# A new order of 1190 planned steps, other engines for 47 evacuations, and a new table of array parts

## The chip, the cores and the metric

The kernel runs on one core of one Trainium2 chip. Five engines work side by side on it: TensorE (PE; matmuls and transposes, with weight loads on PEld beside them), VectorE (DVE), ScalarE (ACT), GpSimd (POOL) and SyncE (SP), which here issues most of the DMAs. The metric is device microseconds of one execution; lower is better. Each engine takes its own instructions strictly in the order in which the program gives them and waits on semaphores for what it needs from the others.

## The reference

One input `x` of 2048 rows by 640 channels is normalised over its channels. The normalised rows go two ways: through a gated long convolution (A) and through a feed-forward net (B). The product of the two, through a SiLU, is added to `x`.

```python
def _A_ref(q, k, v, shift_k, ssm_k, ssm_D):
    ...
    for t in range(ks):                       # ks = 4
        k_shift = k_shift + k_pad[:, t:t + S, :] * shift_k[:, ks - 1 - t][None, None, :]
    kv = k_shift * v
    ...
    kv_f = rfft(kv, padded to 2 S)            # S = 2048
    kf_f = rfft(ssm_k, padded to 2 S)
    y = irfft(kv_f * kf_f)[:S] + kv * ssm_D
    return q * y

def _B_ref(x, w1, b1, w2, b2):                # 640 -> 1728 -> 640
    return einsum(gelu(einsum(x, w1) + b1), w2) + b2

xn = layernorm(x)
return x + _A_ref(xn, k, v, ...) * silu(_B_ref(xn, ...))
```

(The two transforms are shortened to words here.) B_x is not used.

## The kernel before

The long convolution is done by a transform of length 4096 split into two stages. The first stage multiplies 128 x 128 matrices of cosines and sines (`WA`, `WB`) onto the rows; the second multiplies 32 x 32 matrices (`mats`) onto blocks of 32 rows; between the two stages the data change places through DRAM. So there are three trips through DRAM: `scrK` (the filter's spectrum), `scrU` (the signal's) and `scrC` (the product on its way back). On each trip all 16 stores have to land before any of the 16 loads can run, because each load reads a stripe of every store.

The feed-forward net runs over four chunks of 512 rows. Chunk 0 is taken up by a fixed opening (`prologue`), which also does the first six hidden blocks of that chunk. Everything after it is a list of 1190 names, `PLAN`, that is read from left to right; each name calls one small function and issues its instructions. The order of the list is thus the order on every engine's queue and on SP's and GpSimd's DMA queues. Nothing else orders the work: an engine that reaches an instruction too early waits there, and everything behind it on that engine waits too.

The names that matter here (a number is the piece, `.a` or `.d` says ScalarE or VectorE):

- `h`, `he`: one hidden block of 128 features of the feed-forward net, five matmuls of 512 columns (L463; every 14th, `h13 h27 h41 h55`, is a narrow one, L459), and its gelu on ScalarE (L475, L472). Numbers 0 to 13 are chunk 0, 14 to 27 chunk 1, and so on.
- `g`, `ge`, `gm`: one output half-block, 14 matmuls of 320 columns (L496), its SiLU on ScalarE (L504), the product on VectorE (L511). A `g` needs all 14 `he` of its chunk and all of `w2_sb`.
- `ls lv lr lb ln`: layernorm (statistics L417, L418 on VectorE; the root on GpSimd L426; the normalisation on ScalarE L438 or VectorE L440). `tt`, `te`: four transposes of normalised rows (L447), evacuation.
- `em`, `ee`: matmuls that spread the four taps over the partitions (L641), evacuation into `w_exp`. `cv`: one multiplication, addition or product with `v` of the short convolution, on VectorE (L590, L586, L579), eight to each of eight pieces.
- `w`, `ws`: phases and sines that fill `WA` and `WB`; `s ss sm` the same for `mats`; `d` adds `ssm_D` into the filter (L638).
- `kt`, `kc`: five transposes of one sixteenth of the filter, one from each of its five loads (L535), evacuation. `kf`, `ke`, `ks`: first stage of the filter (L546), evacuation, store to `scrK` on GpSimd's queue (L561). `uf`, `ue`, `us`: the same for the signal (L546, L572).
- `fl`: load of a `scrK` pair on SP (L595). `ff`, `fe`: 32-row unit of the filter's second stage, evacuation. `ml`: load of a `scrU` pair (L652). `mk`: two loads that swap even and odd partitions of the filter's spectrum (L658). `mu`: 32-row unit of the signal. `mp`, `mq`: two products of spectra on VectorE, straight from PSUM (L670). `ma`, `mb`: the two 32-row units of the inverse, into one bank. `me`: evacuation. `ms`: store to `scrC` (L700).
- `ip ia is ib ic`: `WA` and `WB` are filled anew for the way back. `yl`: load of `scrC` (L707). `y`, `yt`: last stage (L715, L716) and product with the normalised rows (L724). `yo`, `ys`: addition of `x` and store for the first three chunks; `ga`, `gs` for the last.
- `X B C K V q`: loads of `x`, `w2`, the filter, `k`, `v`, and `x` again (L238, L272 to L275, L268, L243 to L245, L248, L704), all on SP. `B2` is three small loads, `C` five of 512 KB.

Two kinds of storage are handed out while the list is read: eight PSUM banks (`ones`) and 48 row-pair slots of one large SBUF tile (`slots`). Both are first-in-first-out: a step that opens a new piece takes the one that has been free for longest, and the step that uses a piece for the last time gives its place back. So a new order also changes which bank and which slot each piece gets, and on whose last use it waits. In the opening the six blocks of the prologue hold banks 0 to 5, and 6 and 7 are free.

The second-stage units (`ff mu ma mb`, 192 in all) use a 32 x 32 corner of the array for each block of rows, four matmuls a unit. The digit of `TURNS` for the unit's number (0 to 47) says which column block is paired with which row block (L408 to L410): digit t pairs block i with i+t. Forward units (`ff`, `mu`) and inverse ones (`ma`, `mb`) swap the roles of the two, so units whose pairings differ can run in the array at the same time.

All evacuations go through one helper (`evac`), L146 where ScalarE does it and L147 where VectorE does it. ScalarE keeps one table of functions loaded: gelu, or SiLU, which serves the sines too; `use_table` issues a change where the list demands one.

Of the kernel before, what the change touches and what calls it, by code (L numbers as in the profile page):

```python
# [39 lines left out]
kt4 kt3 kt13 kf25 kt9 kf34 kt2 V6 kc14.a kc3.a kc13.d kc4.d ke34.a kc2.d kt12 kf0 kc9.d kc12.d ke25.a kf33 ke0.a  # L40
ke33.a kt10 kf6 kt7 V4 X2 V0 X3 kf2 kt6 kf7 kf17 kc7.a kc10.d ke6.d kf28 ke2.a kc6.a kf27 kt15 kf29 kt1 ke7.d kf12
ke17.d ke28.a ke29.a kf30 kc15.d kc1.d ke12.d ke27.a kf45 kf35 ke35.a kf15 kf39 kf31 kf20 ke39.a ke15.a kf8 ke30.a
ke45.a ke20.a ke8.a g3 cv33 ks11 ks9 kf13 cv13 cv40 cv23 ke31.d kf26 kf38 ge3 ke13.a ke38.a kf32 ke32.a ke26.a kf41
ke41.a kf47 kf37 gm3.d kf36 ke47.a ke36.a kf3 g4 gm2.d ke3.a ke37.a ge4 kf10 kf40 kf14 kf18 kf16 ke10.a kf19 ke40.a
ke16.a ke14.a ke19.a g5 kf44 kf5 kf46 kf23 kf24 cv14 cv56 cv5 cv34 cv35 cv48 cv24 cv41 cv15 kf1 ks10 ks12 ks2 ks5 ks13
cv42 cv43 gm4.d cv6 cv36 cv7 cv44 ke18.a ge5 ke46.a ke44.a g6 kf21 ks4 ks6 cv37 cv25 cv45 cv38 ke23.a ke24.a ke5.a
ke1.a ke21.a ks8 kf9 ke9.a kf4 kf11 kf22 ke22.a ge6 kf42 ke42.a ke11.a ke4.a g7 kf43 ge7 ke43.a uf4 uf14 ks15 uf3 uf13
ue3.a ue4.a uf12 uf16 uf5 ue14.a ue16.d cv39 ks7 ks0 ks1 ks3 cv46 cv26 cv57 cv49 cv27 ue12.a ue5.a h23 h18 h24 uf2
cv50 cv51 cv47 cv52 cv28 ue13.a he24 he18 uf29 uf9 ue29.a uf8 uf10 ue10.a ue9.a ue8.a h21 uf24 uf6 h16 uf26 ue2.a he23
he21 ue24.a he16 h14 uf1 uf7 ue7.a h26 he14 he26 ue26.a ue6.a uf34 h17 ue34.a uf33 h22 he17 ue1.a cv53 gm6.d cv54 cv58  # L50
cv29 uf28 uf17 h27 uf11 ue28.a he27 he22 h25 ue33.d ks14 fl6 fl4 fl2 fl10 fl12 fl8 fl1 fl5 fl9 cv55 cv59 ue11.a ue17.a
uf0 uf30 ue30.a ue0.d cv30 cv60 h20 he20 uf27 uf41 ue27.a uf35 uf36 h19 uf25 fl3 fl14 ue35.a he25 ue41.a uf38 uf37
fl11 fl0 us1 us4 us11 us2 h15 fl15 ue36.d he19 gm5.d cv31 fl7 ue38.d uf20 uf18 ue25.a uf31 uf23 uf19 he15 ls10 ls9
# [5 lines left out]
lb2 g11 ml4 ml3 ls14 fe34.a ln8.d ln10.d ln9.d ls15 ff25 ff11 ff10 ff5 ff38 ff16 g12 ge11 fe5.a fe10.a fe11.a fe25.a  # L59
fe16.a ge12 ln11.d fe38.d ff43 ff33 ff19 ff20 tt14 tt12 ff12 ff47 fe33.d fe19.a fe43.a mk3 ml1 fe20.d te14.d te12.d  # L60
tt13 fe12.a fe47.a ff4 fe4.a tt11 ff15 ff3 mu8 gm10.d lv3 mu7 ff26 g14 gm11.d gm12.d te11.a fe3.a fe15.a fe26.a te13.a
mk4 ml8 mk1 mu6 mp7 mp8 mq8 mq7 ma7 ma8 ff32 lr3 mb8 mu11 mu9 mb7 fe32.a lb3 tt10 g13 mk8 me8.a te10.a ln13.a me7.a
mp6 mp9 mq9 mp11 mq11 ml0 fl13 mu12 mq6 mk0 ml6 ff45 ff21 mu3 mu5 ge13 fe45.a ln15.a ge14 mp12 fe21.a mq12 mp5 g15 mq5
ge15 ma12 ff18 ma11 mb12 ma5 mp3 mq3 ml7 mb11 mu4 mu25 mb5 fe18.a me11.a me12.a me5.a h29 mu14 mp4 mu13 mu10 h32 he29
he32 mp25 mq25 mp10 h30 he30 mq10 mq4 mp13 mp14 mq14 mq13 h39 ln12.a mu1 ml5 ff30 ma9 mu26 mb9 ma4 h40 mp1 he39 mq1
fe30.a me9.a he40 mu2 mb4 mu18 ma6 ff39 h28 ml10 mk6 mk5 ml12 ml9 ml13 mk7 me4.a fe39.a mb6 ff36 mu24 mu19 ln14.a mp26
mk9 mq26 mp2 mp18 mq2 h34 h31 mp19 mp24 mq24 me6.a fe36.a he28 mk12 he34 mu15 mu17 mq19 ml14 mq18 he31 ff41 ma10 ma2
ff40 mb2 mb10 mu23 mp17 mq17 fe40.a me10.a me2.a fe41.a h35 h41 he35 mp15 mq15 he41 mp23 mq23 ma13 mu28 ma18 mb18 mu22
mb13 me13.a me18.a mp22 mq22 mp28 h36 he36 ma15 ma1 mb1 mb15 mu16 ma24 mb24 me15.a me1.a me24.a ml11 q6 h37 mp16 mq16
mu21 ma14 ma26 mq28 mb26 mk13 ma16 mb16 mb14 mu0 he37 q1 mu38 h38 me14.a me16.a me26.a he38 mp21 mq21 mp38 mp0 mq0 h33  # L70
mq38 ma19 ma0 q3 mk11 mk14 q7 ma3 mu27 mk10 gm14.d mu37 mu40 mb3 mb19 he33 mb0 tt18 te18.a me3.a me19.a me0.a g17 mp40
mp27 mq40 mq27 tt15 tt19 mp37 gm13.d mu20 mu34 mu41 mq37 g16 te15.a te19.a mp20 mp41 mq20 mq41 ma28 ma38 ma40 mu43
mb28 mb38 mb40 tt17 mk15 mp34 ml15 ge16 ge17 te17.a gm16.d mp43 gm17.d gm15.d g18 mu29 me38.a me40.a me28.a mq34 ma25
mu35 ma34 ma27 mb34 mu31 mb25 ge18 ms0 ms4 ms1 ms2 mb27 mq43 tt16 me34.a me27.a me25.a te16.a mp29 mp31 mp35 mq29 mq31
g19 ir mu39 ma29 mu36 ma17 ma31 ge19 mu32 mb29 mb17 mb31 mq35 me17.a me31.a me29.a ms5 g20 mp36 mq36 mp39 mq39 ma23
mu45 ma36 ma37 mb23 ma21 mb37 mb36 ge20 mu30 mb21 mp32 mq32 g21 ma20 mp30 me37.a me36.a me21.a me23.a mu47 ma39 ms3
ma41 mp45 mq30 mu33 ma30 mq45 gm19.d mb41 mb39 mb20 mb30 me39.a gm18.d me20.a g22 me41.a q0 ma43 mp33 mp47 q2 mq33
me30.a ge21 mq47 ma22 ma33 mu44 mu46 ma47 mb33 mb22 ge22 mb43 h53 me43.a me22.a ms9 mp44 me33.d mp46 mq44 ma32 ma35
# [828 lines left out]
```

## Time and profile before

| quantity | value |
|---|---|
| time, median of 3 runs | 196.9 us (196.85 to 197.02) |
| span of the profiled execution | 195.1 us |
| TensorE busy | 186.0 us, 95% of the span |
| VectorE busy | 174.9 us, 90% |
| ScalarE busy | 161.8 us, 83% |
| GpSimd busy | 49.3 us, 25% |
| moved by DMA | 57.69 MB, mean 296 GB/s |
| changes of ScalarE's table behind the opening | 7 |

The profiled execution is one run of the same program with the hardware profiler on; its span goes from the first instruction to the last. Start times in the rows are counted from the span's start. In rows that group instructions, "x14" is the number of instructions, and the name behind "<-" in brackets is what the engine last waited for. A TensorE row's length contains the time in which a matmul is still on its way through the array, so rows overlap; in the chain of work that ended last the overlaps are taken out. The granted clock is TensorE's, 1.00 for full speed.

### The profile page before, as it was taken

To read this page: it belongs to the slowest core of one execution; us is meant where nothing else is said; L and a number is where in the kernel's file an instruction comes from. 1 tells how busy PE (TensorE), PEld (TensorE's weight loads), DVE (VectorE), ACT (ScalarE), POOL (GpSimd) and SP (SyncE) were. 2 spreads that over 40 slices of the span, in tenths; PEclk is the share of its full clock that TensorE was granted. 3 is DMA by queue.
4 is the path that set the end of the run, shared out by engine and by line. 5 is a ranking of instruction groups with operands and counts; after the bars stand their busy time and mean duration, and the time that the engine had idled before them with its cause. 6 is when DMAs were issued, how large, how long until landed. Compare 5 with 4: busy or idle time off the path is not lost.

```text
span 195.1 us, 5140 instructions
## 1 busy us (share of the span) xinstructions
PE 186.0 (95%) x1927; PEld 110.8 (57%) x1939; DVE 174.9 (90%) x374; ACT 161.8 (83%) x320; POOL 49.3 (25%) x85
## 2 busy tenths in 40 slices
PE   7899979899999999999999999999999999999992
PEld 2486447776775555563556433356665454676771
DVE  6969999999999999999999999999999910479994
ACT  3467999989999999999998999989867699993031
POOL 8545300003555000635020000008073610002130
PEclk9999999999999999999999999999999999999999
DMA  6999999983599899987699998599897659994064
GB/s 199 386 363 312 348 392 404 401 349 154 202 368 364 292 337 364 397 328 288 235 300 307 312 363 295 174 281 352 254 304 304 238 190 315 369 392 186 5 234 171
DMA packets 26401, 57.69 MB, mean 296 GB/s; under 512 B 3016, under 2 KB 14857, under 8 KB 26376
## 3 DMA queue, kind: packets, MB, share of 16 engines
q1 hardware_dynamic: 21872, 39.65, 59.4%
q0 software_dynamic: 4320, 17.70, 24.1%
q8 instruction: 15, 0.25, 0.5%
q14 instruction: 10, 0.08, 0.1%
q10 hardware_dynamic: 184, 0.01, 0.1%
HBM read 33.76 MB, written 18.35 MB: 267 GB/s over the span
## 4 chain that ended last, share of the span: by engine, by line
PE 78%; DVE 16%; issue 2%; POOL 1%; ACT 1%; POOLq 0%; DVEq 0%; ACTq 0%
PE banks L496 28%; PE banks L463 22%; PE banks L546 9%; PE banks L410 9%; DVE area L590 3%; PE banks L535 2%; PE banks L715 2%; PE banks L716 2%; DVE area L586 2%; DVE st L417 2%; PE banks L447 2%; DVE stats L744 1%; DVE area L303 1%; DVE area L147 1%; DVE xnT L147 1%
## 5 line engine op out<-in xcount | busy, mean ns | idle before, releaser
L146 ACT CAST area<-banks 128x426 bf16<-128x426 f32 (+2 forms) x169 | 76.7, 570 | 5.4 <-PE banks L410 4.3
L496 PE MATMUL banks<-w_sb,hT 128*128 128x320 bf16 (+1 forms) x462 | 65.5, 295 | 0.0
L463 PE MATMUL banks<-xnT,w_sb 128*128 128x512 bf16 x218 | 53.2, 380 | 0.7 <-issue 0.2
L496 PEld LDWEIGHTS <-hT 128*128 128x128 bf16 x462 | 43.5, 98 | 18.2 <-issue 2.2
L670 DVE TENSOR_TENSOR area<-banks,area 128x426 bf16<-128x426 f32 (+1 forms) x96 | 49.9, 591 | 0.4 <-PE banks L410 0.4
L475 ACT ACTIVATE hT<-banks,b_f 128x512 bf16<-128x512 f32 x52 | 34.2, 708 | 2.5 <-PE banks L782 1.4
L463 PEld LDWEIGHTS <-w_sb 128*128 128x128 bf16 x230 | 21.3, 98 | 25.6 <-issue 3.6
L504 ACT ACTIVATE sl<-banks 128x320 bf16<-128x320 f32 (+1 forms) x33 | 14.7, 456 | 13.7 <-PE banks L496 11.2
L590 DVE TENSOR_TENSOR area<-area 128x1280 bf16<-128x1280 bf16 x32 | 24.8, 813 | 0.2
L700 POOL DMA_DIRECT2D scrC<-area x16 | 11.7, 733 | 41.6 <-ACT area L146 41.4
L410 PE MATMUL banks<-area,mats 32*32 32x426 bf16 (+1 forms) x768 | 20.9, 345 | 0.5
L724 DVE TENSOR_TENSOR area<-banks,xn 128x426 bf16<-128x426 f32 (+1 forms) x18 | 10.2, 592 | 12.3 <-ACT hT L475 11.3
L586 DVE TENSOR_TENSOR area<-area 128x1280 bf16<-128x1280 bf16 x24 | 18.9, 812 | 0.0
L561 POOL DMA_DIRECT2D scrK<-area x16 | 8.8, 555 | 29.7 <-ACT area L146 29.7
L546 PE MATMUL banks<-area,WA 128*128 128x428 bf16 (+1 forms) x64 | 16.1, 298 | 0.2
L410 PEld LDWEIGHTS <-mats 32*32 32x32 bf16 x768 | 8.1, 88 | 12.7 <-issue 9.6
L546 PE MATMUL banks<-area,WB 128*128 128x214 bf16 (+1 forms) x64 | 15.1, 299 | 0.0
L147 DVE CAST area<-banks 128x426 bf16<-128x426 f32 (+2 forms) x27 | 14.9, 583 | 0.0
L572 POOL DMA_DIRECT2D scrU<-area x16 | 8.6, 539 | 22.6 <-ACT area L146 20.7
L733 POOL DMA_DIRECT2D out_dram<-area x6 | 3.3, 547 | 28.6 <-DMA area<-in_A_q_dram 19.3
L417 DVE BATCH_NORM_STATS2 st<-xn 128x6 f32<-128x320 bf16 x24 | 10.3, 470 | 0.0
L511 DVE TENSOR_TENSOR xn<-xn,sl 128x320 bf16<-128x320 bf16 (+1 forms) x33 | 9.7, 308 | 0.4 <-ACT sl L504 0.4
(107 smaller groups left out, 202.3 us busy)
## 6 DMA issues: line engine op xcount, KB each, us to landing
scrK<-area POOLq DMA_DIRECT2D x16, 320.0 KB, 3.5
scrU<-area POOLq DMA_DIRECT2D x16, 320.0 KB, 4.0
area<-scrK SPq DMA_DIRECT2D x16, 320.0 KB, 6.0
area<-area SPq DMA_DIRECT2D x32, 160.0 KB, 4.1
area<-scrU SPq DMA_DIRECT2D x16, 320.0 KB, 5.9
scrC<-area POOLq DMA_DIRECT2D x16, 320.0 KB, 4.2
area<-scrC SPq DMA_DIRECT2D x16, 320.0 KB, 7.4
area<-in_A_k_dram SPq DMA_DIRECT2D x4, 640.0 KB, 8.2
```

Source lines behind the costliest of these rows:

```text
L146: return nc.scalar.copy(out=out_ap, in_=in_ap)
L147: return nc.vector.tensor_copy(out=out_ap, in_=in_ap)
L410: nc.tensor.matmul(out=out[b, :], lhsT=mats[a, m, a], rhs=rhs[a, :], start=start, stop=stop)
L417: nc.vector.bn_stats(out=st[:, j, h, :], in_=xn_tiles[c][:, j, h * HALF:(h + 1) * HALF])
L463: nc.tensor.matmul(out=ps, lhsT=w1_sb[:, t, ft * P:(ft + 1) * P], rhs=xnT[:, t, :], start=(t == 0), stop=(t == DT - 1))
L475: nc.scalar.activation(out=hT[:, ft, :], in_=one(("h", i)), func=ACT.Gelu_apprx_tanh, bias=b1_f[:, ft:ft + 1], scale=1.0)
L496: nc.tensor.matmul(out=ps[:, 0:ws.stop - ws.start], lhsT=hT[0:M, ft, q * P:(q + 1) * P], rhs=w2_sb[0:M, ft, hs.start + ws.start:hs.start + ...
L504: nc.scalar.activation(out=sl[:, ws], in_=one(key)[:, 0:ws.stop - ws.start], func=ACT.Silu)
L546: nc.tensor.matmul(out=ps[:, dst], lhsT=(WA, WB)[r][:, n2, :], rhs=rows[:, n2 % 2, src], start=True, stop=True)
L586: nc.vector.tensor_tensor(out=uc, in0=uc, in1=tmp, op=ALU.add)
L590: nc.vector.tensor_tensor(out=tmp if s else uc, in0=kh[:, r0:r0 + KC, :], in1=w_exp[:, j:j + 1, :].to_broadcast([P, KC, D]), op=ALU.mult)
L670: nc.vector.tensor_tensor(out=flat(("p", i))[:, x * w:x * w + w], in0=one(("mu", i))[:, 0:w], in1=flat(key)[:, cols(j)], op=ALU.mult)
```

## The change

The list has the same 1190 names (engine choices aside, none is added or lost), in another order from its first name on. 47 of the names that can go to either engine change it: 26 from VectorE to ScalarE (`fe` 7, `ke` 5, `ue` 5, `kc` 4, `te` 2, `me` 2, `ee` 1) and 21 from ScalarE to VectorE (`kc` 5, `ue` 5, `fe` 5, `te` 2, `me` 2, `ke` 1, `ln` 1). The table of array parts is another one. ScalarE changes its table nine times behind the opening, not seven. The opening itself and all functions stay as they are.

```diff
-TURNS = "331023121031002102313332203331230123011120302102"
+TURNS = "023103310231110031233032212101001210031323322122"
 
 PLAN = """
-h11 s X1 he0 he2 w h13 em5 em6 he4 he3 em4 he1 he5 em7 ee7.a ee5.a he11 h9 K1 K0 ls7 ls4 ls6 ls5 ee6.d lv1 cv16 h6 B0
-B1 B2 ee4.a he9 he13 he6 cv8 lr1 cv17 lb1 cv9 h12 h8 h7 he12 ln5.a he8 cv0 cv1 ln7.d cv10 ln4.d ln6.d h10 cv18 cv19 C3
-tt7 tt5 tt8 tt6 he7 he10 g0 tt9 g1 te6.d te5.d te8.d cv20 C1 C0 C4 C2 ws0 ss ge0 cv2 cv11 cv3 sm cv21 te9.d ws1 ge1
-te7.a g2 ws2 gm0.d cv12 gm1.d d K2 kt8 kt11 V2 V3 V1 cv22 cv4 ge2 kc11.a kc8.a V7 K3 kt5 kc5.d kt0 kt14 V5 kc0.d cv32
...
+em6 X1 K0 K1 em5 ls4 w ls5 he0 em4 he1 he2 ls7 ls6 cv17 ws1 em7 ee7.a h13 h10 he3 he13 ee5.a he5 B2 lv1 h8 B0 ee4.a lr1
+he10 cv9 cv0 cv1 s h9 ee6.a he8 B1 he4 cv2 h7 lb1 cv8 C0 h11 he7 ln6.d h6 cv16 he9 cv3 ln5.a he11 C3 h12 C1 he6 he12 ss
+ws0 cv18 C4 ln7.d cv19 g6 ln4.d ge6 tt6 cv10 tt8 C2 cv20 sm g2 ge2 cv21 V0 kt11 kt13 cv11 te8.d kc13.a kt3 kt4 kt10 kt2
+kc3.d kc10.d kt9 kc4.a kc2.d V7 kc11.a kt7 kc9.d ws2 kt14 K2 kf11 ke11.a cv12 kt1 d kt5 kc14.d te6.d kc7.d kt6 cv4 cv22
+kc5.a g5 ge5 tt5 kc1.d te5.a kt0 kf27 kc6.d kc0.a kt12 kt8 kc8.d tt9 kc12.d kf34 ke27.a kf43 kf33 te9.d ke34.a kf5
...
```

The middle of the list, where the signal's first stage ends and the filter's second stage runs:

```diff
...
-fe14.a us12 us3 us6 us0 uf40 uf32 ge9 ue32.a us5 us10 uf21 ue23.a ue40.a us13 us8 ue21.a fe1.a g10 cv63 gm7.d gm9.d
-ls8 ge10 ls12 uf47 uf45 ue45.a ue47.d uf44 uf42 uf43 ue42.a uf46 ue43.a lv2 ue46.d ff8 ff9 ff37 ff24 ff2 us15 fe37.d
-ue44.a fe9.d fe24.a uf22 ff28 ff22 ff6 ff46 fe2.a fe22.a fe8.a ue22.d ff27 fe28.d fe6.a ff7 ff35 ff17 ff34 fe27.d
-fe7.d fe35.a ff29 fe29.a ff44 fe44.a ff42 fe42.a ff31 ff23 fe46.a fe31.a mk2 us14 us7 ml2 ls13 fe23.d gm8.d fe17.a lr2
...
+fe26.d uf46 ue46.d ue43.a ue47.d uf45 ue45.a ff10 us14 ff6 fe17.a ff37 fe10.a ff27 gm14.d fe37.d ff25 ls12 fe27.a fl0
+ff2 fe2.a ff4 fe4.a g11 ff45 ff1 fe6.a ls15 fe25.a ff11 ff18 ge11 fe45.d ff5 ln10.d ff35 fe35.a ff9 fe5.a g9 us4 gm8.d
+fe11.a ls13 ff32 ff14 fe1.d fe18.a fe9.a ff36 ge9 us15 ff28 ff33 ff13 mk2 tt12 tt10 fe14.d ff30 fe32.a fe33.d ff12
+fe36.a tt13 te12.d tt14 fl7 fe13.a fe28.a te10.d lv3 ff42 gm13.d ml2 ml3 gm9.d fe30.a te13.a ff21 mu6 mp6 mq6 ml4
...
```

And the passage from the inverse's last units to the last stage, and the end:

```diff
...
-mu42 mb47 mb32 mb35 me32.a q5 h43 h49 mq46 mp42 me35.a me47.d mq42 ma42 ma46 ma45 ms12 ms8 ma44 ms13 mb42 mb46 mb45
-ip1 ms7 me45.a me46.a ms11 ms10 ms6 ms15 mb44 me44.a me42.a ms14 h44 h51 g23 h47 h46 ia1 gm20.d is1 ib1 ic1 he53 he46
-he47 h48 he48 h45 h55 h50 he51 he45 he49 he55 he50 h54 he43 he54 h42 he42 he44 yl5 yl4 h52 y6 he52 ip0 ip2 ip3 ia0 is0
...
-gm28.d ge29 ge30 ys1 ge31 gs27 gs25 gm30.d gm29.d ga30 gs30 ga28 ga29 gs29 ys3 ys5 gm31.d ga31 gs31 ys4
...
+h55 h43 me41.a mq17 me44.a me45.a mp17 ms9 mq42 mp42 ma42 ms13 ms12 ma17 ib1 ma46 ma31 mb42 mb17 me17.d mb46 ip0 ic1
+mb31 me31.a ia0 me46.a g20 h45 me42.d gm19.d he55 ga31 ms10 he48 ms5 h47 h50 he47 ms14 ia3 h54 h42 ge20 gm20.d h44 is3
+q6 ms15 yl5 he54 h51 yl9 yl7 gm16.d ip2 he44 he42 h49 h46 yl6 ib3 yl4 he49 he46 yl10 q3 he43 he51 h53 he53 he45 ia2
+yl15 y11 h52 y9 yt9 he52 he50 y7 y6 y8 yt8 yt11 yt7 g24 yl8 yl12 y10 ic3 yl13 is2 yt6 yt10 g26 yl14 yo2.d is0 y20 ib0
...
+ys0 y5 g27 y23 ga25 ga24 gs25 yt5 y16 yo1.d yt16 ys4 ge29 ge27 gm27.d yo5.d ys1 ga27 g30 ge30 yt23 ga26 gm29.d ga29 g28
+ge28 gm30.d gs27 gm28.d ga30 ga28 ys5 gs29 g31 ge31 gs30 gm31.d gs31
```

More of the change, by code (lines that the diff above doesn't have):

```diff
@@ L39 @@
-te7.a g2 ws2 gm0.d cv12 gm1.d d K2 kt8 kt11 V2 V3 V1 cv22 cv4 ge2 kc11.a kc8.a V7 K3 kt5 kc5.d kt0 kt14 V5 kc0.d cv32
[L40 to L53, printed above, removed]
@@ L59 @@
[L59 to L73, printed above, removed]
@@ L74 @@
[L74 to L78, printed above, removed]
@@ new lines @@
+he23 us1 cv30 lv2 lr2 he25 uf24 ue30.a uf29 fe24.a cv61 cv31 ue29.a cv62 g13 uf38 us0 fe7.a uf26 uf32 ue32.d fl3 uf41
+ge13 fl5 ue41.d g14 ue38.a ue26.a us12 ue24.a us8 us13 uf19 ge14 uf12 ue19.a ls14 uf27 ue27.a uf18 uf14 uf21 ue14.a fl9
+lb2 us10 ue21.d ln11.d uf20 ue18.a ue20.a fl10 ln9.d g8 cv63 ff20 ue12.a us6 fe8.a ff44 ff31 ff46 ff38 ln8.d uf22 uf44
+ge8 uf47 us9 fe31.a uf42 fe20.d ue22.d fe44.a ue44.a ff43 fe38.d uf23 fe46.a ue23.a ue42.a ff17 ff26 fe43.d uf43 us7
+fe26.d uf46 ue46.d ue43.a ue47.d uf45 ue45.a ff10 us14 ff6 fe17.a ff37 fe10.a ff27 gm14.d fe37.d ff25 ls12 fe27.a fl0
```

37 lines of the change are left out of this document (32 added, 5 removed).

## The prediction

> **What bounds the kernel now.** I read the page's head, then busy time by stretch, then TensorE's rows in order of time, then the chain of work that ended last. By stretch (busy us of PE, PEld, DVE, ACT, POOL with instruction counts; granted clock, DMA share, GB/s):
>
> ```profile
> span 195.1 us, 5140 instructions
> ```
>
> ```profile
> 13.84:36.90 23.06, 21.30 (x175) 14.10 (x175) 22.48 (x47) 21.41 (x32) 5.11 (x5) 1.00 1.04 364
> 36.90:120.20 83.30, 82.29 (x836) 47.51 (x844) 82.92 (x164) 81.69 (x177) 19.59 (x34) 1.00 0.88 313
> 120.20:153.80 33.60, 33.44 (x597) 18.11 (x581) 33.18 (x69) 26.98 (x58) 11.10 (x19) 1.00 0.80 267
> 153.80:189.50 35.70, 35.49 (x243) 22.43 (x241) 23.26 (x50) 23.76 (x41) 5.41 (x9) 1.00 0.68 244
> ```
>
> Three engines are full at once. Up to 120.2 (about TensorE's last `ff`) VectorE idles 0.58+0.38 us and ScalarE 1.65+1.61; from there to the last `mb` near 153.8 TensorE and VectorE are full; behind it TensorE alone. The median of the runs shown is 196.9, so 1.8 us lie outside this execution's span; I carry them over.
>
> TensorE's busy time hides waits, so next its own rows (start, length, idle before and releaser in brackets):
>
> ```profile
> 16.58 1.03 PE L463 MATMUL banks<-xnT,w_sb 128*128 128x512 bf16 x4
> ...
> 26.55 1.31 PE L447 MATMUL banks<-ident,xn 128*128 128x128 bf16 x16 [1.05 <-DVE xn L440]
> ...
> 35.33 1.78 PE L535 MATMUL banks<-ident,area 128*128 128x128 bf16 x25 [0.59 <-DVE area L638]
> ...
> 89.70 3.34 PE L410 MATMUL banks<-area,mats 32*32 32x426 bf16 x56
> ```
>
> And its pace, from the chain (start, length, line, matmuls):
>
> ```profile
> 37.29 0.31 PE banks L535 x5
> ...
> 44.07 1.90 PE banks L496 x14
> ...
> 49.58 1.09 PE banks L546 x10
> ...
> 76.61 1.08 PE banks L463 x5
> ...
> 97.56 0.48 PE banks L410 x16
> ...
> 99.29 0.29 PE banks L410 x4
> ...
> 119.82 0.91 PE banks L410 x36
> ...
> 143.25 0.71 PE banks L410 x40
> ...
> 153.30 0.51 PE banks L410 x32
> ```
>
> One `h` costs 1.08, one `g` 1.90, one `kt` 0.31, one `kf` or `uf` 0.18 (six in 1.09). A stretch of 32-row units costs 0.29 for one unit, 0.48 for four whose array parts (0,1,1,3) need two rounds, 0.71 for ten that need three, 0.51 for eight that need two: 0.29 and about 0.2 for each further round. (One of nine units in three rounds took 0.91.) So the stretch at 89.70, 14 units in seven rounds and thus 1.5, lost about 1.8 us of its 3.34: its evacuations could not follow. Between 35.33 and 44.07 stand 13 `kt` and 20 `kf`, 7.6 of 8.7: 1.1 lost. With 1.05 and 0.59 TensorE lost some 4.5 to 5 us behind 16.58. That is all a better order can win there: it would end near 190. A worse one has no such bound.
>
> **The change, part by part.**
>
> *TURNS.* I count rounds in program order: a forward unit with digit t takes part t, an inverse one part -t mod 4, and a unit waits while its part is in use. Old order with old table: 69 rounds in 29 stretches. New order with new table: 69 in 29. The new order with the old table would need 102, which is 33 x 0.2 = 6.6 us more: the table belongs to the order, and by itself gives nothing. Every other TensorE step is the same in number. TensorE's work changes by 0; what changes is when it waits.
>
> *47 choices.* 26 go to ScalarE, 21 to VectorE. Net, ScalarE gets `ke` +4, `fe` +2, `ee` +1, `kc` -1, `ln` -1, VectorE the reverse. Prices from the groups by line (busy us over count) and from one full stretch of each engine:
>
> ```profile
> L475 ACT ACTIVATE hT<-banks,b_f 128x512 bf16<-128x512 f32 x52 | 34.2, 708 | 2.5 <-PE banks L782 1.4 <-PE banks L463 1.0
> ...
> L438 ACT ACTIVATE xn<-xn,nb,rs 128x640 bf16<-128x640 bf16 x5 | 4.7, 940 | 0.0
> ```
>
> ```profile
> 87.94 7.30 ACT L146 CAST area<-banks 128x428 bf16<-128x428 f32 x17
> ...
> 88.97 3.65 DVE L147 CAST area<-banks 128x426 bf16<-128x426 f32 x7
> ```
>
> An evacuation is 0.43 on ScalarE and 0.52 on VectorE, a gelu 0.66, an `ln` 0.94. In front of the last `ff`, ScalarE has six evacuations and an `ee` more (2.6 and, at the same price, 0.4); two `ln` (1.9), one `he` (0.7) and one `kc` (0.6, row below) fewer: 0 in all, to 0.2. VectorE has six evacuations (3.1), one `mp` and one `mq` (1.0) fewer; `ln`, `gm`, `kc` one more each and `ee` one fewer, +0.7 at the evacuation's scale: -3.4. TensorE has one `h` fewer there, -1.1, paid back later.
>
> *The opening.* Here the order differs most. Old: seven `h`, four `tt`, `g0 tt9 g1 g2`, then `kt8`. New: taps, `h13 h10 h8 h9 h7 h11 h6 h12 g6 tt6 tt8 g2`, then `kt11`: three `tt` and one `g` fewer stand in front of the first `kt`. A `kt` reads all five filter loads (C, L268); W2 (L274 last) is needed by the first `g`. Issue times and time to landing:
>
> ```profile
> L274 SPq DMA_DIRECT2D w_sb<-in_B_w_dram x1: 1711/1711/1711, 17.0 to 17.0; - x1
> ...
> DMA to landing us min/median/max: 9.8/9.8/9.8
> ```
>
> ```profile
> L268 SPq DMA_DIRECT2D area<-in_A_ssm_k_dram x5: 328/356/430, 19.2 to 24.9; - x5
> ...
> DMA to landing us min/median/max: 8.6/9.1/9.5
> ```
>
> W2 is in at 26.8, the filter at 24.9+8.6 = 33.5 at the earliest. Old `kt8` came just then. The DMA share of this stretch is 1.04, and the same loads stand ahead of the last C on SP's queue in both orders, so I keep both times. New TensorE: 16.58 + 0.6 (four taps) + 0.7 (`h13`) + 7 x 1.08 = 25.4, and 0.5 of waiting, since `h10` takes the bank that `ee7` frees behind the moved `ws1`: 25.9. `g6` waits 0.2 for W2 and ends at 28.0; two `tt` (16 transposes in 1.31, so 0.3 each) and `g2`: 30.5. **Then TensorE waits 3.0 us for the filter.** The other two run dry as well:
>
> ```profile
> 26.25 1.28 ACT L314 ACT_TABLE_LOAD   x1
> ...
> 33.04 2.02 ACT L328 ACTIVATE WA<-area,sin_bias_h 128x2048 bf16<-128x2048 f32 x1
> ...
> 35.27 2.48 ACT L146 COPY area<-banks 128x640 bf16<-128x640 bf16 x4
> ```
>
> ```profile
> 36.65 0.87 DVE L147 COPY area<-banks 128x640 bf16<-128x640 bf16 x2
> ...
> 43.40 2.27 DVE L590 TENSOR_TENSOR area<-area 128x1280 bf16<-128x1280 bf16 x3
> ```
>
> Old ScalarE reached its first `kc` at 35.27. In front of the new one stand no `ws2` (2.0), one `ge` and one `te` fewer (0.9), one `ee` more (0.4), and `ws1` fills 1.3 of its early idle: 31.5; `kt13` is evacuated from about 34.1, so 2.6 to 2.9 idle. Old VectorE reached its first `kc` at 36.65; in front of the new one stand three `cv` (0.76 each), three `te`, an `ee`, two `gm` and `d` fewer (some 2 in all): about 32, and `kt3` comes at 34.6: 2.6 idle. What goes for it: the waits of 1.05 and 0.59 (`kt0`, the only one that `d` holds, is now late).
>
> *To the last `ff`.* ScalarE: work 0, idle 0.3+2.9 in the opening and, I take, 0.4 later (bounds 0 and the 1.61 of before; near the low end, since its early `kc` waits now lie in the hole) against 3.26: +0.3. VectorE: work -3.4, idle 2.6+0.4 against 0.96: -1.4. ScalarE decides: 120.5. TensorE has 1.1 less done there, so it ends 1.4 late.
>
> *The middle barrier.* All `us` stores must land before the first `ml` load:
>
> ```profile
> scrU<-area POOLq DMA_DIRECT2D x16, 320.0 KB, 4.0
> ...
> area<-scrU SPq DMA_DIRECT2D x16, 320.0 KB, 5.9
> ```
>
> 4.0+5.9 and the issues are 11 us by the medians. Old `uf22` ends and `mu8` starts about that far apart (89.7 to some 100). New: `fl7` stands behind `mk2` on SP, which waits for `fe6`, and `ff21` and `mu6` need `fl7` and `ml2`; by ScalarE's evacuations 9 us lie between `uf45` and `mu6`. What is late next is the load. I take 0, because a load into a quiet queue lands sooner than the median; bounds 0 and 2.
>
> *The end.* The last `scrC` stores and the first loads of them:
>
> ```profile
> 155.12 1.56 POOL L700 DMA_DIRECT2D scrC<-area  x2 [0.62 <-ACT area L146]
> ...
> 159.42 12.61 SPq L707 DMA_DIRECT2D area<-scrC  x16
> ```
>
> Between the last `mb` and the first `y` TensorE has one `g` and ten `h` (12.7; old 12.3). Four stores instead of two follow the last `me`, 1.5 later, but those `me` are split over two engines, 1 earlier. I take +0.1, bounds 0 and 1. Two more table loads (`ge20` among the `he`) cost ScalarE 2 x 1.28 and a little, where it idles 11.9 of 35.7: nothing on the path, up to 0.7 if `g24` has to wait for `he50`. The last microseconds keep their order (`g31 ge31 gm31 gs31`).
> The Trainium skill's "ScalarE: Activation LUTs" (Step-by-step: what each stage is for) puts a table load at about 2.7 us with its drain; by it the two would cost 5.4, still inside that idle, and the trace's 1.28 decides.
>
> Sum: 195.1 + 1.4 + 0.1 = 196.6 of span, and with the 1.8 outside it **198.4 us**.
>
> **Rivals.**
> *Paid back (faster).* The hole is there, but behind it TensorE waits for nothing: VectorE's 3.4 and `ff` stretches of seven units instead of 14 take the evacuation waits away. Then its waits are 0.7+3.0 and about 0.5 against 5: 195.1 - 0.8 + 1.8 = 196.1, and 195.6 if the last `ff` also goes without any. For it: 3.4 us less on the fullest engine. Against: ScalarE's work there is the same, and it must not idle at all from 34 to 119; that is the point from which it decides.
> *Cancel.* The filter comes a microsecond or so sooner than in this trace, and the rest holds: 197.0.
> *The clock.* At its start TensorE was slow, although the granted clock reads 9 in every slice:
>
> ```profile
> PEclk9999999999999999999999999999999999999999
> ```
>
> ```profile
> 1.36 2.74 PE L764 MATMUL banks<-ident 128*128 128x512 bf16 x6 [1.36 <-POOL ident masks.py:199]
> ...
> 4.65 1.92 PE L764 MATMUL banks<-ident 128*128 128x512 bf16 x7
> ```
>
> Six 512-column matmuls took 0.46 each, later ones 0.22 (1.08 for five). If a wait of 3 us brings that pace back for some 4 us, 2 us of work are lost: 200.4. No wait of before behind the start was over 1.1 us, so its trace does not exclude it.
> The Trainium skill's "TensorE: Matmul & The Clock Gate" (HAM oscillation — how this bites in real kernels) has the clock halve after idle gaps of over some 3.4 us; by that rule 3.0 just escapes.
> *The table misses the array's parts.* Then rounds are not the law and up to 6.6 us come on top; the rows of 0.29, 0.48, 0.51 and 0.71 speak against it, and I give it no share of its own.
>
> **How the numbers follow.** Forecast (197.4 to 199.6) 0.45; clock, or late loads at a barrier, 0.11; cancel 0.17; paid back 0.27. So faster by over 0.2% 0.27, within 0.2% 0.17, slower 0.56; 0.2% (0.4 us) is about what a measurement of this kernel can tell from no change. The range takes in the paid-back case and the clock: 195.6 to 200.4.
>
> **What would show it.** Right: in the profile after, TensorE at the first `kt` (L535) waits 2 to 3 us near 31 for the `in_A_ssm_k` loads, VectorE and ScalarE idle beside it, the last `ff` comes near 120.5, the 32-row stretches keep 0.29 to 0.71, and ScalarE stays full while VectorE has some idle. Wrong: the first `kt` runs at 31 without a wait, the last `ff` comes before 118.5, or the first `y` waits over 1 us for `scrC`.

## The result, and the profile after

After takes 202.9 us (median of four runs, 202.0 to 204.4) against 197.0 for before beside it: ratio 1.030, 95% interval 1.025 to 1.035, so 5 to 7 us slower. The forecast was 198.4 with 195.6 to 200.4: the sign was right, the size was not. The ratios and their intervals leave out the executions that the record marks as slow, while the medians are of all executions, so a ratio can lie below what its median says. The profiled execution of after is the fastest of its four (202.0 us). Its span is 200.2 us against 195.1, so 5.1 us have to be found in it.

TensorE's rows of after in order of time, as in the prediction (start, length, idle before and releaser in brackets), those with a wait, without two of 0.24 and 0.37 at 59 and 72 us:

```profile
17.75 7.71 PE L463 MATMUL banks<-xnT,w_sb 128*128 128x512 bf16 x34 [0.20 <-ACT area L146]
...
28.39 0.62 PE L447 MATMUL banks<-ident,xn 128*128 128x128 bf16 x8 [1.02 <-DVE xn L440]
...
31.41 1.78 PE L535 MATMUL banks<-ident,area 128*128 128x128 bf16 x25 [0.38 <-DMA area<-in_A_ssm_k_dram]
...
101.01 0.37 PE L410 MATMUL banks<-area,mats 32*32 32x428 bf16 x8 [1.10 <-DMA area<-scrU]
...
119.49 0.39 PE L410 MATMUL banks<-area,mats 32*32 32x426 bf16 x12 [0.99 <-DMA area<-scrU]
...
134.02 0.36 PE L410 MATMUL banks<-area,mats 32*32 32x426 bf16 x4 [1.03 <-DVE area L670]
...
157.57 0.58 PE L410 MATMUL banks<-area,mats 32*32 32x428 bf16 x32 [0.41 <-DVE area L670]
...
173.18 0.26 PE L715 MATMUL banks<-area,WA 128*128 128x212 bf16 x1 [0.41 <-DMA area<-scrC]
```

The wait of 3.0 us that I had put at the first `kt` is 0.38. Instead there are waits between 101 and 134 us, where before has none. VectorE's rows of after with a wait (one of 0.23 at 112 us left out), from the first product to the last:

```profile
101.50 2.13 DVE L670 TENSOR_TENSOR area<-banks,area 128x428 bf16<-128x428 f32 x4 [1.83 <-PE banks L410]
...
118.62 2.63 DVE L670 TENSOR_TENSOR area<-banks,area 128x426 bf16<-128x426 f32 x5 [1.26 <-PE banks L410]
...
132.86 1.11 DVE L670 TENSOR_TENSOR area<-banks,area 128x426 bf16<-128x426 f32 x2 [0.91 <-PE banks L410]
...
155.39 2.13 DVE L670 TENSOR_TENSOR area<-banks,area 128x426 bf16<-128x426 f32 x4
```

and the same stretch of before, where the largest row holds 52 products without a gap:

```profile
100.72 2.11 DVE L670 TENSOR_TENSOR area<-banks,area 128x426 bf16<-128x426 f32 x4
...
102.89 26.68 DVE L670 TENSOR_TENSOR area<-banks,area 128x428 bf16<-128x428 f32 x52
...
149.13 0.60 DVE L670 TENSOR_TENSOR area<-banks,area 128x426 bf16<-128x426 f32 x1 [0.40 <-PE banks L410]
...
152.70 0.59 DVE L670 TENSOR_TENSOR area<-banks,area 128x428 bf16<-128x428 f32 x1
```

From the first product's start to the last one's end before takes 52.6 us (100.72 to 153.29) and after 56.0 (101.50 to 157.52). VectorE waits 2.4 us inside it in after and 0.4 in before; the rest of the difference is other work of VectorE.

To see where TensorE loses, I reckon its lost time at each `g`: the time since the opening's end (16.6 in before, 16.2 in after) less the work that the list puts in front of that `g`, at the prices of the prediction, but with a stretch of 32-row units as 0.36 + 0.05 for each unit. That makes the column an estimate. For after's `g18`: 134.3 - 16.2 - 106.7 = 11.4.

| up to about | before: at, lost | after: at, lost |
|---|---|---|
| the end of the first eight `g` | `g7` 56.5, 3.1 | `g1` 54.2, 2.3 |
| the first `ff` | `g8` 80.3, 3.5 | `g13` 79.3, 3.8 |
| the last `us` | `g11` 93.0, 6.3 | `g9` 94.8, 5.4 |
| the first products | `g15` 106.1, 6.6 | `g10` 107.2, 7.8 |
| the middle of the products | `g17` 130.1, 6.9 | `g18` 134.3, 11.4 |
| the last `mb` | `g23` 155.9, 6.5 | `g20` 158.1, 11.7 |
| the last `g` | `g31` 189.2, 6.7 | `g31` 194.5, 12.4 |

Up to 95 us after is about one microsecond ahead. It then loses 2.4 us around the first products (2.0 of them up to `g15`, which starts at 101 in after), **3.6 us between 107 and 134**, and 1.0 behind that; before loses 0.3, 0.3 and nothing there. Of the 3.6, TensorE's rows show 2.0 as waits (0.99 and 1.03); the rest lies inside rows. The array parts do not explain it: counted as in the prediction, after needs 24 rounds there and before 23 in its like part. The experiments go for these two places.

### The profile page after: what moved, and what is told of

The parts are those of the page before. It is cut to its first block, busy times and chain, and to the rows that moved or that the text cites. A ratio compares the mean times of both kernels' runs of the same rounds, so it can differ in the third digit from the quotient of the medians.

```text
span 200.2 us, 5129 instructions
## 1 busy us (share of the span) xinstructions
PE 187.8 (94%) x1928; PEld 111.5 (56%) x1939; DVE 173.5 (87%) x369; ACT 165.9 (83%) x328; POOL 51.0 (25%) x85
## 4 chain that ended last, share of the span: by engine, by line
PE 35%; DMA 26%; ACT 19%; DVE 12%; SPq 3%; issue 3%; POOL 0%; DVEq 0%; POOLq 0%; ACTq 0%
PE banks L496 17%; ACT area L146 13%; DMA w_sb<-in_B_w_dram 9%; DMA area<-in_A_ssm_k_dram 5%; PE banks L410 5%; PE banks L463 5%; DMA area<-scrU 4%; ACT hT L475 3%; DVE area L670 3%; DMA area<-scrC 3%; PE banks L535 3%; DVE area L724 2%; DMA scrU<-area 2%; DMA xn<-in_A_q_dram 2%; DVE area L147 2%
## 5 line engine op out<-in xcount | busy, mean ns | idle before, releaser
L146 ACT CAST area<-banks 128x426 bf16<-128x426 f32 (+2 forms) x176 | 80.4, 614 | 3.9 <-PE banks L410 3.4
L504 ACT ACTIVATE sl<-banks 128x320 bf16<-128x320 f32 (+1 forms) x33 | 15.7, 479 | 17.7 <-PE banks L496 16.2
L410 PE MATMUL banks<-area,mats 32*32 32x426 bf16 (+1 forms) x768 | 21.4, 345 | 3.8 <-DMA area<-scrU 2.1
L700 POOL DMA_DIRECT2D scrC<-area x16 | 11.7, 731 | 48.5 <-ACT area L146 47.1
L546 PE MATMUL banks<-area,WB 128*128 128x426 bf16 (+1 forms) x64 | 16.0, 299 | 0.0
L546 PE MATMUL banks<-area,WA 128*128 128x212 bf16 (+1 forms) x64 | 15.4, 299 | 0.3 <-DVE area L147 0.2
L572 POOL DMA_DIRECT2D scrU<-area x16 | 8.8, 550 | 16.6 <-ACT area L146 16.5
L147 DVE CAST area<-banks 128x426 bf16<-128x426 f32 (+1 forms) x20 | 11.3, 592 | 1.5 <-PE banks L410 0.9
```

Source lines behind the costliest of these rows:

```text
L146: return nc.scalar.copy(out=out_ap, in_=in_ap)
L147: return nc.vector.tensor_copy(out=out_ap, in_=in_ap)
L410: nc.tensor.matmul(out=out[b, :], lhsT=mats[a, m, a], rhs=rhs[a, :], start=start, stop=stop)
L504: nc.scalar.activation(out=sl[:, ws], in_=one(key)[:, 0:ws.stop - ws.start], func=ACT.Silu)
L546: nc.tensor.matmul(out=ps[:, dst], lhsT=(WA, WB)[r][:, n2, :], rhs=rows[:, n2 % 2, src], start=True, stop=True)
```

## The experiments

### Is it the barrier?

Theory 1: the signal's loads come too late behind the barrier, and everything to 135 us follows from it. Rivals: the 47 choices (2), the table (3). The first edit lets the loads read the filter's scratch, which is complete long before:

```diff
-        nc.sync.dma_start(out=pair(("uin", g2), 3), in_=pair_view(scrU)[g2])
+        nc.sync.dma_start(out=pair(("uin", g2), 3), in_=pair_view(scrK)[g2])
```

> After, with the second-stage loads of the signal (ml) reading the filter's scratch scrK in place of the signal's scrU, so that the middle barrier is gone (the signal's values are then wrong; the work is the same). Theory 1 (the loads of the signal come too late, and what TensorE and VectorE lose at 95 to 135 us follows from that): 202.9 falls by 3 to 5 us, to 198 to 200; mu2 no longer waits, and TensorE's idle between g11 and g18, 6 us now, falls below 3. Theory 2 (the 47 engine choices bind ScalarE or VectorE at 108 to 135): falls by less than 1, to 202 to 203. Theory 3 (array parts): no change.

203.2 us (ratio 1.033, 1.031 to 1.035): nothing gained. TensorE still loses 2.1 us around the first product and 3.8 in the middle. **Theory 1 falls as it stood.**

> Before, with the same edit: ml reads scrK in place of scrU, the middle barrier is gone (the signal's values are wrong, the work is the same). Theory 1: before loses almost nothing at this barrier, 196.2 to 197.2 against 197.0. If it falls by 2 us or more, the barrier binds both kernels alike and theory 1 doesn't explain their difference.

196.8 (0.9987 to 1.0005): before loses nothing at that barrier either.

### Choices and table without the order

> After's order and table with before's choices of ScalarE or VectorE for the 47 evacuations. Theory 2 (the new choices cost the time): falls by over 2 us, to 198 to 201. Theory 1 (loads too late, whatever the choices): within 1.5 of after, 201.5 to 204.5.

212.4 us (1.072 to 1.085): 9.5 slower than after.

> Before's order and table with the new choices for the 47 evacuations. Theory 2: 199 or more, since the choices cost by themselves. Theory 1: 196.5 to 198.5, the choices are worth a microsecond or so in a list that they were not fitted to.

210.6 us (1.068 to 1.071): 13.7 slower than before. The first lies above what either theory said. The second lies far above theory 1 and is, as a number, what theory 2 allowed (199 or more); but theory 2 also needed after to gain by the old choices, and it lost 9.5. So **theory 2 falls**: the choices do not cost the time, and they are worth far more than their sum of work says, but only in the list for which they were chosen. Two rows of TensorE in the run of before's list with the new choices, and of after's list with the old ones, show what a wrong choice does:

```profile
60.30 0.34 PE L546 MATMUL banks<-area,WB 128*128 128x426 bf16 x1 [2.65 <-ACT area L146]
```

```profile
67.70 5.08 PE L464 MATMUL banks<-xnT,w_sb 128*128 128x512 bf16 x15 [2.18 <-DVE area L148]
```

In the second, the evacuation stands behind additions and multiplications of the short convolution on VectorE, which has no pause there from 59 us on. In the first, ScalarE itself had stood idle for 4.11 us and goes on at 59.73, just when VectorE ends a `cv` at 59.65; by the list this is `cv15`, which gives back the slot that the evacuation `ke23` takes. Either way an evacuation that comes late holds a bank, and TensorE stands. (The second row also shows 15 matmuls in 5.08 where 3.2 is the pace; that is the clock, below.)

> After with before's table of array parts; nothing else changes. Theory 3 (the table must fit the order, as the count of rounds says: 69 rounds with the new table, 102 with the old one, 0.2 us each): 202.9 rises by 4 to 7, to 207 to 210. If the parts hide behind other engines in this stage, it rises by under 2.

206.6 us (1.044 to 1.051), 3.7 over after and just below the 207 to 210 expected: by TensorE's lost time 0.8 more between `g10` and `g18` and 2.8 between `g18` and `g20`. The table must fit the order; a round is worth about 0.1, not 0.2 (3.7 over 33). By the count of rounds 12 of the 33 fall between `g10` and `g18` and 19 between `g18` and `g20`, so a round cost some 0.07 where TensorE waits for others anyway and 0.15 where it does not.

### What holds the first product

SP's rows of after around the barrier (L658 is `mk`, L595 `fl`, L652 `ml`):

```profile
94.03 1.56 SPq L658 DMA_DIRECT2D area<-area  x2
95.68 0.54 SPq L595 DMA_DIRECT2D area<-scrK  x1
97.47 1.77 SPq L652 DMA_DIRECT2D area<-scrU  x3
```

`mk2` waits for an evacuation until 94, `fl7` stands behind it, `ml2` behind both. `ff21`, which reads `fl7`, stands directly in front of `mu6`, the first signal unit. So even without the barrier the first product cannot come sooner. Theory 5 puts this together with VectorE's rows: its 96 products set the stretch from the first one on, and SP's order made the first one late. Three runs move names on SP's queue (barrier taken away as above):

```diff
-... fl0 ff2 ... mk2 tt12 ... fl7 ... gm13.d ml2 ml3 gm9.d ... mq6 ml4 ...
+... ml2 ml3 ml4 fl0 ff2 ... mk2 tt12 ... fl7 ... gm13.d gm9.d ... mq6 ...        (e6)
+... fl0 ff2 ... ml2 ml3 mk2 tt12 ... fl7 ... gm13.d gm9.d ... mq6 ml4 ...        (e11)
+... fl0 ff2 ... fl7 ml2 ml3 mk2 tt12 ... gm13.d gm9.d ... mq6 ml4 ...            (e16)
```

> After, with ml reading scrK in place of scrU (no middle barrier; the signal's values are wrong, the work is the same) and with ml2 ml3 ml4 moved in front of fl0, so that they no longer stand behind mk2 and fl7 on SP. Theory 5 (VectorE's 96 products bind from the first one on, and SP's order, not the barrier, made the first one late): the 1.8 us of VectorE's idle time ahead of the first product go to under 0.5, and the time falls by 1.5 to 2.5 below the 203.2 of the run without the barrier alone, to 200.5 to 202. Theory 1 alone (the barrier): no change against 203.2.

209.6 us (1.040 to 1.060), worse than expected by either theory: the three loads now stand in front of `fl0`, and TensorE waits for it with `ff2`:

```profile
97.26 0.37 PE L411 MATMUL banks<-area,mats 32*32 32x426 bf16 x8 [3.04 <-DMA area<-scrK]
```

> After, with ml reading scrK in place of scrU (no middle barrier; the signal's values are wrong, the work is the same) and only ml2 ml3 moved in front of mk2 and fl7, four places. Theory 5 (SP's order in front of the first product): the 2.0 us in which VectorE waits ahead of the first product fall under 0.5 and the time falls by 1 to 2 below 203.2, to 201.2 to 202.2. If the first product is late for another reason (the list has too little work ahead of it), it stays within 0.5 of 203.2.

203.3 us (1.030 to 1.034): no gain, VectorE still waits 1.6 us. `fl7` is still behind `mk2`.

> After with ml reading scrK in place of scrU (no middle barrier; the signal's values are wrong, the work is the same) and with fl7, ml2 and ml3 all in front of mk2. ff21, which needs fl7, stands directly in front of mu6. Theory 7 (fl7 behind mk2 on SP holds ff21, and with it mu6 and the first product): TensorE's wait there (1.1 to 1.3) and VectorE's idle time ahead of the first product (1.6 to 2.0) fall under 0.5, the time falls by 1 to 2, to 201.3 to 202.3. If it stays at 203.2, the gap is refilled later by the waits at 118 and 133 us.

202.1 us (1.016 to 1.028, against 1.031 to 1.035 without this move): 1.1 us won by the medians and 2.1 by the ratios (1.022 against 1.033). VectorE's first product follows without a wait,

```profile
98.75 0.55 DVE L512 TENSOR_TENSOR xn<-xn,sl 128x320 bf16<-128x320 bf16 x2
99.35 2.37 DVE L671 TENSOR_TENSOR area<-banks,area 128x428 bf16<-128x428 f32 x4
```

and TensorE's lost time there falls from 2.0 to 0.2 us. So it takes both: the barrier, which lets `ml2` go at 97.5, and `mk2`, behind which `fl7` goes at 95.7 and `ml2` no sooner. Without the barrier alone nothing was won, and with `fl7` moved but the barrier kept (below, together with the two products) neither.

> After with eight ff (ff20 ff44 ff31 ff46 ff38 ff43 ff17 ff26) and their fe moved behind the last ue, so that the last store to scrU is issued about 2 us earlier (91.9 now). If the barrier is the first cause (theory 1): ml2 is issued 1 to 2 us earlier and the time falls by 1 to 2, to 201 to 202. Since the run without the barrier gained nothing, I expect no gain: 202 to 204; the filter's units then come later and mk2 with them.

203.9 us (1.023 to 1.041): `ml2` goes out 1.2 us earlier, counted from `g13` (97.3 - 80.3 against 97.5 - 79.3), and nothing is won.

### Two products that read a refilled bank

The waits of 1.26 and 0.91 us on VectorE at 118 and 133, and TensorE's 1.03 right behind the second, have the same lengths in after, in the run without the barrier and in the three runs with the loads moved (to 0.01). The code says why:

```python
        slots.drop(key)
        if x:                       # x = 1 is mq
            ones.drop(("mu", i))
```

The bank of a signal unit is given back by `mq`, in the belief that `mq` comes after `mp`. In before's list it always does. In after's list 26 of the 48 units have `mq` first. For 24 of them nobody takes the bank before `mp` has read it. Twice somebody does:

```diff
...
 mq25 ff39 ml13 he33 ma10 mq3 me24.a ff23 mp3 he28 mu2 fe39.a mp25
...
 mq28 ms1 h32 mq21 mu18 me2.a he29 mp21 mu22 ms8 me35.a ma21 ma20 mb20 mp28
...
```

`ff23` gets the bank of `mu25` and `mu22` that of `mu28`, so `mp25` and `mp28` wait for these and multiply their output: in after two of the 96 products are formed from another unit's values.

```diff
-... mq25 ff39 ... fe39.a mp25 ... mq28 ms1 ... mb20 mp28 ...
+... mq25 mp25 ff39 ... fe39.a ... mq28 mp28 ms1 ... mb20 ...
```

> After with mp25 directly behind mq25 and mp28 directly behind mq28 (seven and eight products' or other steps' places earlier); banks are given out as in after, but both products now read their own unit. Theory 6: VectorE's waits of 1.26 and 0.91 and TensorE's of 1.03 go, the time falls by 1.5 to 2.5, to 200.4 to 201.4. If the waits come from the order of TensorE's steps and not from the bank: 202.3 to 203.5.

202.7 us (1.021 to 1.031, after 1.025 to 1.035): no difference in time that the runs can tell. The waits of 0.91 and 1.03 are gone, as expected; the one of 1.26 is replaced by a longer one beside the same place:

```profile
121.19 1.11 DVE L671 TENSOR_TENSOR area<-banks,area 128x426 bf16<-128x426 f32 x2 [1.44 <-ACT area L147]
```

```profile
120.73 0.39 PE L411 MATMUL banks<-area,mats 32*32 32x426 bf16 x12 [1.35 <-DMA area<-scrU]
```

TensorE waits here for `ml0`, late on SP's queue, which issues almost without a pause from 97 us on, and VectorE's next two products are those of `mu2`, which reads `ml0`.

> After with the bank of a signal unit given back by the later of its two products, not by mq; mp25 and mp28, which in after read the outputs of ff23 and mu22, then read their own unit. Every later piece may get another bank. Theory 6 (the early return makes the waits of 1.26 and 0.91): both go, 202.9 falls by 1.5 to 2.5, to 200.4 to 201.4, unless the new banks bring waits of their own.

202.9 us (1.025 to 1.036). The waits of 0.91 and 1.03 are gone, at 119 VectorE waits 0.94 in place of 1.26, and TensorE's loss between `g10` and `g18` falls from 3.6 to 2.5; but other banks bring other waits to TensorE (1.00 at 119, 0.63 at 144, both for L146).

> After with both: ml reads scrK in place of scrU (no middle barrier; the signal's values are wrong, the work is the same) with fl7, ml2 and ml3 in front of mk2, and mp25 and mp28 directly behind mq25 and mq28. If late loads and the two products that read a refilled bank are what the stretch from the first to the last product loses: it falls from 56.0 to 53 to 54 us (before: 52.6), VectorE's idle time in it below 0.8, and the time to 199.5 to 200.7. If the order of the steps itself costs it: the stretch stays above 55 and the time at 201.5 or more.

203.2 us as a median (1.024 to 1.033), with a spread of 200.2 to 204.7. In the profiled execution, its fastest, the first product again follows without a wait, and the loss from `g10` to `g18` is 3.0. The stretch of products stays at 55.9 us (99.45 to 155.36), not 53 to 54, so the two repairs are not what the stretch loses. What came out is the other branch, above 55 us and 201.5: the order of the steps itself, whatever in it that is. In place of the old waits VectorE has, among others, 0.68 for `mk`'s loads and 0.85 in front of the products of `mu2`.

> The run before (mp25 and mp28 directly behind their mq) with fl7 in front of mk2, the barrier kept. fl7 then no longer delays ff21, but ml2 still waits for the stores to scrU until 97 us: 0 to 1 us less than with the two products alone, 199.8 to 201.2.

> After with the eight ff behind the last ue (earlier last store to scrU), fl7 in front of mk2, and mp25 and mp28 directly behind their mq; the barrier kept, all values right. ml2 was issued at 97.3 us in the run with the earlier store alone, so the loads still start late: 201 to 203. A gain of over 2 us against 202.9 would say that the barrier is not what holds the loads here.

204.6 us (1.022 to 1.035) and 203.5 us (1.029 to 1.037), both above what was expected: the lists with the barrier kept win nothing back. No list of these runs beats before.

### Is it VectorE's work, or the traffic?

> After with ip0 ip1 ip3 ia0 ia1 is1 ib1 ic1 moved behind me42.d, so that VectorE's 3.1 us of index work (three L617 of 0.68 and one L621 of 0.42 between products, and one of 0.62 ahead of the last evacuation) no longer stand among the products and ahead of the last store to scrC. Theory 5 (VectorE binds from the first product to the last evacuation): the time falls by 1.5 to 3, to 200 to 201.5. If that stretch is set by something else (TensorE's order, loads): within 0.7 of 202.9, or later, since the sines of the way back come later.

205.5 us (1.042 to 1.045). Three of the moved steps stood between `g18` and `g20`, 1.8 us of VectorE. Without them that part takes 23.6 us (135.2 to 158.8), with them 23.8 (134.3 to 158.1): VectorE idles instead. So its work does not set that part, and **theory 5 falls** in so far as it says so. There was little to win there: by the table TensorE loses only 0.3 us between `g18` and `g20` in after; of the part between 107 and 134, where none of the moved work stood, this run says nothing. The later index work made TensorE wait 1.28 and 1.26 us at 166 and 172 for gelus behind later table loads.

> After without the 32 loads of mk: the second product takes the filter's spectrum itself in place of its swapped copy (other values, the same work on the engines; 5.1 MB and 32 issues on SP less). Theory 5 with SP's queue and the DMA engines as what makes VectorE idle: the three idle times of VectorE between 99 and 134 us (4.0 us together) shrink below 1.5, and the time falls by 2.5 to 4.5, to 198.5 to 200.5. If they stay, it is the order of the steps itself (in-order latency from mu to me) and the time stays within 1 of 202.9.

205.5 us (1.029 to 1.046). Without `mk` and its 32 loads the waits in front of the first product (2.18), at 121 (1.21) and at 136 (0.91) are all still there, so the traffic of `mk` does not explain them. The last two are those of `mp25` and `mp28`, which no load can take away. Between `g10` and `g18` TensorE needs 26.6 us instead of 27.1, so that traffic is worth no more than some 0.5 there in this run.

### The opening

> Before with B2 (three small loads) ahead of B0 and B1 on SP, as the new order has it; nothing else changes. If the order of these loads is why the filter landed at 31.4 in after and at 33.5 in before: the filter lands at 31 to 32.5, TensorE's wait in front of the first kt falls by 1 to 2, and the time falls by 0.5 to 1.6, to 195.4 to 196.5. If it is the place of C in the list or the traffic: 196.8 to 197.2.

197.1 us (0.9988 to 1.0016). With `B2` first SP issues the last of the filter's five loads at 22.4, before at 25.2, and the first `kt` starts at 33.63 as before at 33.64. So the order of these small loads does let the filter go sooner, and in before's list nothing waits for it.

> After with the step w (VectorE's phases of the first stage's matrices) in front of ls4, two places earlier; nothing else. In the profiled run of after TensorE waited 0.2 us behind the opening, in five other profiled runs with the same opening 1.3 to 1.8, because ls4 on VectorE waited for its rows of x, w stood behind it, and ScalarE's L326 and the evacuations behind w. Theory: the wait falls to 0.2 or less in every run and the time from 202.9 to 201.8 to 202.4. If the start is set by another wait: 202.5 to 203.3.

203.9 us (1.032 to 1.036). The wait for L146 behind the opening is gone, and the two `tt` wait 1.38 us for VectorE's L441, 1.02 in after: no gain.

## Why the prediction was right or wrong

*The opening.* TensorE reached the first `kt` at 30.75 (forecast 30.5). **The wait behind it failed**: 0.4 us instead of 3.0. The step that failed is "the same loads stand ahead of the last C on SP's queue in both orders, so I keep both times". The same loads, but in another order; SP issued C from 14.6 to 21.0 us, not from 19.2 to 25.2, and the run with `B2` first shows that this order alone moves the last issue by 2.8.

*To the last `ff`.* Forecast 120.5 for TensorE; by the list it stands in the stretch at 120.99, just ahead of the narrow `h` at 121.77. The figure is near by luck: the forecast put the loss into the opening, and the trace has TensorE 1 us ahead at 95 and behind by 107. "ScalarE decides" fails too, since VectorE idles from 99 and ScalarE from 102 on.

*The middle barrier.* The mechanism was named as it is: "`fl7` stands behind `mk2` on SP, which waits for `fe6`, and `ff21` and `mu6` need `fl7` and `ml2`". The size was wrong: I took 0 of bounds 0 and 2, because a load into a quiet queue lands sooner. The load did (3.5 us), but the stores did not: their median landing was 5.5 us, in before 4.0, with a DMA share of 0.89 from 90 to 100.5 us, in before 0.75. The chain of the work that ended last has the two (start, length):

```profile
92.43 4.88 DMA scrU<-area
...
97.47 3.50 DMA area<-scrU
```

It cost 2.0 of TensorE's time, the upper bound, and 1 to 2 us of the run in the experiment that took it away.

*What had no term.* The sum has 0 for the barrier and nothing for what TensorE loses among the products: behind the last `ff` I let it run as in before. Between 107 and 134 it lost 3.6 us where before loses 0.3, by the same estimate about 1.6 of them ahead of the narrow `h` behind the last `ff` and 2.0 behind it. This is the step that, with the 2.0 of the barrier, put the result outside the range. Part of it is the two products on refilled banks: with the bank given back by the later product the loss falls by 1.1. I read `mq` and `mp` as neighbours in whatever order and did not ask which of them gives the bank back. TensorE's 0.99 at 119 is a wait for a load, `ml0`; but without the barrier the loss there is 3.8, and with the loads moved as well about 3.7, so late loads by themselves are not shown to be a part. With both repairs it is 3.0: removing one wait lets the next take its place. Some of the rest may be work. In the run with both repairs VectorE has 24.60 and ScalarE 24.69 us of work between `g10` and `g18`, against 23.69 and 22.83 in about the like stretch of before (columns: length, busy us of PE, PEld, DVE, ACT, POOL; clock, DMA share, GB/s):

```profile
105.30:131.90 26.60, 25.36 (x374) 10.48 (x371) 24.60 (x50) 24.69 (x49) 2.26 (x3) 1.00 0.92 313
```

```profile
106.50:130.20 23.70, 23.44 (x357) 9.98 (x360) 23.69 (x48) 22.83 (x45) 0.00 (x0) 1.00 0.88 280
```

VectorE's surplus is in the list: an `ln` and a `gm` more, 0.8 us by their rows (0.44 and 0.31). ScalarE's is not: both lists give it 44 instructions there, and before merely leaves four of them to the next stretch. So at most about 1 of the 3 us left is work, which is argued and not shown. The other 2 **stay open**: no run of these separates them.

*The 47 choices.* "ScalarE 0, VectorE -3.4" as sums of work may stand, but the sums say nothing of the time: the same choices cost 13.7 us in the other list.

*TURNS.* Right in kind: the table belongs to the order and gives nothing by itself. Its price was 6.6 and is 3.7.

*The end.* Forecast +0.1 with bounds 0 and 1; from the last `mb`'s end to the span's end before takes 41.3 us (153.8 to 195.1) and after 42.1 (158.15 to 200.2): +0.8. The first `y` waited 0.41 for `scrC`. The added table loads take 1.28 each, and TensorE waits for nothing beside this one:

```profile
163.07 1.28 ACT L316 ACT_TABLE_LOAD   x1
```

*The rivals.* "Paid back" needed ScalarE not to idle at all from 34 to 119, and it idles 1.7 us from 102 on. "Cancel" had its premise right, the filter came 2 us sooner (31.4), but the rest did not hold. "The clock" was right as a mechanism and absent from the profiled execution; it shows in other executions, below.

## What to carry to other kernels

Price a new order where the engines hand work to each other, not by sums over engines: a list, its engine choices and its table of array parts are one object, and a part of it taken alone cost 4 to 14 us here. When a list is reordered, ask of every shared buffer which step gives it back and whether that step is still the last reader; here two waits that kept their lengths from variant to variant were the sign of such a false hand-over. And where two waits end together, such as a barrier and a queue behind it, take both away before judging either.
